# Softmax of the first two batches by tensor-engine transposes and row-spreading products

## The chip, the cores and the metric

The kernel runs on one core of one Trainium2 chip. TensorE (PE) multiplies, VectorE (DVE) and ScalarE (ACT) work elementwise, SyncE (SP) issues the DMAs; GpSimd (POOL) only fills constants. Each engine takes its instructions in the order written. The metric is the device time of one execution in microseconds, the median of several. A difference in percent is taken against the kernel before.

## The reference

```python
# x: (8 batches, 8 heads, 512 tokens, 64), state: (8, 8, 32 states, 64)
scores = matmul(x, state.T) / 8
a = exp(scores - scores.max(-1));  a /= a.sum(-1) + 1e-9     # softmax over the 32 states
xread = matmul(a, state)
scores2 = matmul(state, x.T) / 8                             # the same scores, transposed
a2 = exp(scores2 - scores2.max(-1)); a2 /= a2.sum(-1) + 1e-9 # softmax over the 512 tokens
sread = matmul(a2, x)
x = concat([xread, sread], tokens)          # (8, 544, 8*64) -> 4352 rows of 512
h = relu(x @ w_in1);  x = (s*h*h + b) @ w_out1               # 512 -> 2048 -> 512
h = relu(x @ w_in2);  out = (h*h) @ w_out2
```

## The kernel before

The matmuls of the two layers run in a rounded fp32 form, with each operand split in a high and a low part, so that a product takes three passes (high by high, high by low, low by high). Weights come as 64-bit words; ACT takes the magnitude of a piece (line 126), four DVE instructions turn it into fp32 (`to_f32`, lines 135 to 146), and the split follows.

**Attention.** Scores of a batch lie as two tiles (r = 0, 1) of 128 rows by 512 tokens; the rows are four heads by 32 states. So the softmax over tokens runs along a row, and the softmax over states across 32 rows. `att_exp` (line 351) does both: for the tokens a maximum along the row (355) and an exponential with its sum (360); for the states a 32 by 32 block transpose on DVE (358), a maximum (362), a subtraction (363) and an exponential (364). `att_norm` takes the sums and divides (369 to 376); `att_an` transposes the states' softmax back (382), rounds it to the high part (ACT, 384) and takes the low part (DVE, 387). `att_tp` transposes the tokens' softmax on PE (393), and `att_sr` (413) multiplies it by x.

**First layer.** The 64-wide product with the state is folded into the weights: S = state by w_in1 (`s_mm`, `s_first`), so that a step needs six passes `h <- aT, S` (line 448). A step (j, f) is one block of 128 hidden columns of batch j: `mm1` (six passes, 448), three ACT instructions for the squared relu and its high part (455 to 457), the low part on DVE (461), and two steps later `mm2` (twelve passes, 478), which sums into four PSUM banks. The order is steps 0 to 3 of batch 0, steps 4 to 7 of batch 1, then the other 12 of each, then the other batches.

**Order of the work.** It is written out by hand: before the loop over steps come the loads, the scores and softmax of batch 0 and the scores of batch 1; in step i come `mm1`, `early` (conversion of the piece of w_out1 or w_in1 that is due, the pieces of S, the low parts of the step before, relu, magnitudes of the next pieces), `mm2` of step i-2, and then what `at_step(i, fn, rank)` has put there, sorted by rank. Batch 1's softmax stands at steps 0 to 4 (list `first`): exponentials at 0, division at 1, transposes at 2, `att_sr` at 4. Batches 2 to 7 follow the list `calm`.

**Second layer.** Lines 630 to 720, PE products of another arrangement; the change does not touch them.

Of the kernel before, what the change touches and what calls it, by code (L numbers as in the profile page):

```python
# [40 lines left out]
P = 128  # L41
# [20 lines left out]
def attn_mlp2(ctx: ExitStack, tc: tile.TileContext, xT, xn, st, w_in1, w_out1, w_in2, w_out2, s_in, b_in, out):  # L62
# [40 lines left out]
    def x8(shape, name, dt=F32R):  # L103
        return xp.tile(shape, dt, tag="x", name=name)
# [65 lines left out]
    def piece(key, src, q, k):  # L170

        raw = load_piece(key, src, q, k)
        st = {}

        def mag():
            if key == "o1":
                st["v"] = vp.tile([P, 512], F32, tag="v", name="v")
            else:
                if k == 0:
                    V1[q] = w8([P, KD, 512], f"V{q}", F32)  # L180
                st["v"] = V1[q][:, :, k * P : (k + 1) * P]
            magnitude(st["v"], raw)

        def hi():
            nc.scalar.activation(out=w_tiles("o1", q)[0][:, k, :], in_=st["v"], func=ACTF.Copy)

        def lo():
            h, l = w_tiles("o1", q)
            nc.vector.tensor_tensor(out=l[:, k, :], in0=st["v"], in1=h[:, k, :].bitcast(F32), op=ALU.subtract)  # L189

        st.update(key=key, mag=mag, pair=lambda: (st["v"], raw), hi=hi, lo=lo)
        return st
# [137 lines left out]
            )  # L330
        xa[b] = [t, sb, None]

    def att_load_n(b):
        n = x8([P, S // P, DM], f"xn{b}", F32)
        nc.sync.dma_start(out=n, in_=xn[b].rearrange("(t p) d -> p t d", p=P))
        xa[b][2] = n

# [40 lines left out]
    def att_an(b, c, between=None):  # L378
        if c == 0:
            aT_t[b] = x8([P, 2, 2, S], f"aT{b}")  # L380
        an = an1.tile([P, S], F32, tag="an", name="an")
        nc.vector.transpose(out=an, in_=cur[b, c][1].rearrange("p a b -> p (a b)"))
        hi, lo = aT_t[b][:, 0, c, :], aT_t[b][:, 1, c, :]
        nc.scalar.activation(out=hi, in_=an, func=ACTF.Copy)
        if between:
            between()
        nc.vector.tensor_tensor(out=lo, in0=an, in1=hi.bitcast(F32), op=ALU.subtract)  # L387

    def att_tp(b, c):
        sc = cur[b, c][0]  # L390
        tp = pst(f"tp{b}{c}")
        for i in range(4):
            nc.tensor.transpose(out=tp[:, i * P : (i + 1) * P], in_=sc[:, i * P : (i + 1) * P], identity=ident)  # L393
        a2T = (at if b else op).tile([P, 4, P], F32, tag="t1" if b else "o", name="a2T")
        nc.scalar.copy(out=a2T, in_=tp.rearrange("p (a b) -> p a b", a=4))
        cur[b, c] = [a2T]

    def att_turn(b, c):
        att_an(b, c)
        att_tp(b, c)  # L400

    srp_t = {}

# [431 lines left out]
    def later(i, k, loader, rank=0):  # L835
# [12 lines left out]

    calm = ((att_sc, 0, 5), (att_exp, 0, 6), (att_exp, 1, 8), (att_norm, 0, 9), (att_norm, 1, 10),
            (att_an, 0, 11), (att_an, 1, 12), (att_tp, 0, 13), (att_tp, 1, 13), (att_sr, 0, 17), (att_put, 0, 17))  # L850
    first = ((att_exp, 0, 0), (att_exp, 1, 0), (att_norm, 0, 1), (att_norm, 1, 1), (att_turn, 0, 2),
             (att_turn, 1, 2), (att_sr, 0, 4), (att_put, 0, 4))
    rank = {att_sr: 0, att_tp: 0, att_sc: 0, att_put: 2, att_an: 3, att_turn: 3, att_exp: 5, att_norm: 5}
    for b in range(1, B):
        base = step(2, 0) + (b - 3) * NF if b > 1 else 0
        if b > 1:
            at_step(base + 1, lambda b=b: att_load(b), 6)
        at_step(base + 1, lambda b=b: att_load_n(b), 6)
        for fn, c, k in first if b == 1 else calm:
# [151 lines left out]
    with tc.manual_schedule():  # L1011
        make_identity(nc, ident)
        nc.scalar.activation(out=minus, in_=ident, func=ACTF.Copy, scale=-1.0)
        nc.gpsimd.memset(ones, 1.0)
        v0 = [piece("i1", w_in1, 0, 0)]
        att_load(0)
        v0 += [piece("i1", w_in1, 0, k) for k in range(1, VA)]
        nc.sync.dma_start(out=s_sb, in_=s_in.to_broadcast([P, 1]))
        nc.sync.dma_start(out=b_sb, in_=b_in.to_broadcast([P, 1]))
        v0[0]["mag"]()  # L1020
        to_f32(v0[0]["pair"]())
        att_sc(0, 0)
        s_first(0)
        att_exp(0, 0)
        s_first_lo(0)
        att_exp(0, 1)
        for p in v0[1:]:
            p["mag"]()
        att_load_n(0)
        att_load(1)  # L1030
        bring(0)
        bring(1)
        att_norm(0, 0)
        att_norm(0, 1)
        att_an(0, 0, lambda: to_f32(v0[1]["pair"]()))
        att_tp(0, 0)
        att_an(0, 1, lambda: to_f32(*[p["pair"]() for p in v0[2:]]))
        att_tp(0, 1)
        att_sc(1, 0)
# [64 lines left out]
```

## Time and profile before

| what | us |
|---|---|
| median of 3 runs (lowest, highest) | 1407.17 (1406.64, 1409.31) |
| the profiled execution's own time | 1405.25 |
| its span in the trace | 1403.5 |
| PE busy in the span | 1371.6 (98%) |
| DVE busy, ACT busy | 765.1 (55%), 759.1 (54%) |

The profile lists instructions by engine with their start, their duration and, in brackets, how long the engine had been idle before and what released it. A stretch's granted clock of TensorE is given as a share of 2.4 GHz (0.50 is 1.2 GHz). An fp32 matmul appears as two instructions. PEld is the loading of weights into PE. SPq is SyncE's queue of DMA issues.

### The profile page before, as it was taken

The numbers are of one execution on the slowest core, as the hardware profiler recorded it, in microseconds if no ns is written. First come the engines' busy times: TensorE is split into PE (matmuls) and PEld (weight loads), VectorE is DVE, ScalarE is ACT, GpSimd is POOL, SyncE is SP. The second block draws the span as 40 slices with busy tenths as digits, with TensorE's granted clock in tenths as the row PEclk, the third lists the DMA queues.
The fourth block names the chain that finished last, engine by engine and source line by source line (L and its number), as shares of the span: only waits on it lengthen the run. The fifth ranks groups of instructions, "written<-read, shape, count | busy, mean of one in ns | idle before, by whom it ended". The sixth has DMA issues, their size and how long they took to land.

```text
span 1403.5 us, 20210 instructions
## 1 busy us (share of the span) xinstructions
PE 1371.6 (98%) x7770; PEld 1159.5 (83%) x7770; DVE 765.1 (55%) x1495; ACT 759.1 (54%) x1492; POOL 0.7 (0%) x7
## 2 busy tenths in 40 slices
PE   4999999999999999999999999999999999999998
PEld 2677777777777777889988999988999988999897
DVE  7888645555565767345667544453444435343533
ACT  4877656656665656557655543363344335434543
POOL 0000000000000000000000000000000000000000
PEclk9999999999999999999999999999999999999999
DMA  7365232332414241302663655445445544543652
GB/s 239 120 220 184 90 112 73 116 113 85 145 49 143 83 147 60 113 0 98 215 225 138 189 162 160 119 149 158 119 125 172 165 120 120 165 128 108 216 157 68
DMA packets 88863, 188.48 MB, mean 134 GB/s; under 512 B 8640, under 2 KB 26048, under 8 KB 86208
## 3 DMA queue, kind: packets, MB, share of 16 engines
q1 hardware_dynamic: 88768, 187.21, 42.5%
q8 instruction: 61, 1.00, 0.3%
q14 instruction: 34, 0.28, 0.1%
HBM read 144.18 MB, written 42.99 MB: 133 GB/s over the span
## 4 chain that ended last, share of the span: by engine, by line
PE 95%; DVE 3%; ACT 1%; DMA 0%; issue 0%; SPq 0%
PE o L681 27%; PE acc L478 26%; PE m L636 24%; PE h L448 14%; PE S L260 2%; PE sr L413 1%; PE sc L260 1%; PE tp L393 0%; PE S L288 0%; DMA xT<-xT 0%; DVE m L362 0%; DVE t L376 0%; DVE t L363 0%; DVE V L141 0%; DVE V L146 0%
## 5 line engine op out<-in xcount | busy, mean ns | idle before, releaser
L478 PE MATMUL acc<-g,o1h 128*128 128x512 f32 (+1 forms) x1152 | 341.2, 379 | 0.0
L478 PEld LDWEIGHTS acc<-g,o1h 128*128 128x128 f32 x1152 | 211.4, 188 | 41.7 <-issue 2.0
L478 PE MATMUL acc<-g,o1l 128*128 128x512 f32 (+1 forms) x576 | 217.5, 378 | 0.4 <-DVE o1l L189 0.4
L448 PE MATMUL h<-aT,S 128*128 128x512 f32 x768 | 201.9, 397 | 6.2 <-DVE aT L387 3.5
L448 PEld LDWEIGHTS h<-aT,S 128*128 128x128 f32 x768 | 141.4, 189 | 60.9 <-issue 9.2
L636 PE MATMUL m<-xw 128*128 128x384 f32 (+1 forms) x1008 | 183.4, 328 | 2.3 <-DVE r L715 2.3
L636 PEld LDWEIGHTS m<-xw 128*128 128x128 f32 x1008 | 171.5, 188 | 10.0 <-DVE r L715 2.6
L649 ACT ACTIVATE sc<-sc 128x384 f32<-128x384 f32 (+1 forms) x144 | 72.8, 505 | 153.2 <-DVE sc L715 151.7
L461 DVE TENSOR_TENSOR g<-r,g 128x512 fp32r<-128x512 f32 (+1 forms) x144 | 94.8, 658 | 111.0 <-ACT g L457 111.0
L455 ACT ACTIVATE r<-h 128x512 f32<-128x512 f32 (+1 forms) x144 | 82.2, 570 | 124.5 <-PE h L448 123.2
L649 ACT ACTIVATE v<-m 128x384 f32<-128x384 f32 (+1 forms) x96 | 45.5, 474 | 152.8 <-PE m L636 152.2
L478 PEld LDWEIGHTS acc<-g,o1l 128*128 128x128 f32 x576 | 108.4, 188 | 21.1 <-DVE o1l L189 0.9
L681 PE MATMUL o<-o2h,xw('g', 0)_6295 128*128 128x512 f32 x364 | 121.2, 392 | 0.0
L681 PE MATMUL o<-o2h,xw('g', 1)_6296 128*128 128x512 f32 x364 | 121.1, 392 | 0.0
L681 PE MATMUL o<-o2h,xw('g', 2)_6297 128*128 128x512 f32 x360 | 119.7, 392 | 0.0
L715 DVE TENSOR_TENSOR v<-m,r 128x384 f32<-128x384 f32 (+1 forms) x48 | 25.7, 536 | 164.4 <-PE m L636 164.4
L636 PE MATMUL m<-xw,xw('odd', 0)_6176 128*128 128x384 f32 (+1 forms) x576 | 107.4, 328 | 0.8 <-DVE t L715 0.8
L636 PEld LDWEIGHTS m<-xw,xw('odd', 0)_6176 128*128 128x128 f32 x576 | 98.3, 188 | 5.0 <-DVE t L715 1.2
L456 ACT ACTIVATE r<-r 128x512 f32<-128x512 f32 (+1 forms) x144 | 87.7, 609 | 4.6
L457 ACT ACTIVATE g<-r 128x512 fp32r<-128x512 f32 (+1 forms) x144 | 87.6, 609 | 4.6
L111 DVE TENSOR_TENSOR S<-S,S 128x512 fp32r<-128x512 f32 x54 | 34.8, 686 | 91.4 <-ACT S L110 91.4
L636 PE MATMUL m<-xw,xw('odd', 1)_6177 128*128 128x384 f32 (+1 forms) x432 | 79.3, 327 | 0.0
(146 smaller groups left out, 1893.5 us busy)
## 6 DMA issues: line engine op xcount, KB each, us to landing
xw<-w2s SPq DMA_DIRECT2D x140, 256.0 KB, 2.8
xw('odd', 0)_6176<-w2s SPq DMA_DIRECT2D x20, 1024.0 KB, 4.9
xw('odd', 1)_6177<-w2s SPq DMA_DIRECT2D x20, 768.0 KB, 4.3
i1r<-w_in SPq DMA_DIRECT2D x16, 512.0 KB, 5.0
xn<-xn SPq DMA_DIRECT2D x8, 1024.0 KB, 8.8
o1r<-w_out SPq DMA_DIRECT2D x16, 512.0 KB, 4.8
x<-ot SPq DMA_DIRECT2D x32, 256.0 KB, 3.0
i2r<-w_in SPq DMA_DIRECT2D x16, 512.0 KB, 5.3
```

Source lines behind the costliest of these rows:

```text
L111: nc.vector.tensor_tensor(out=lo, in0=src, in1=hi.bitcast(F32), op=ALU.subtract)
L260: nc.tensor.matmul(out=outs[r][k * NS : (k + 1) * NS], lhsT=state[rows, r, k, :], rhs=moving(rows, k), start=True, stop=True, skip_group_c ...
L448: nc.tensor.matmul(out=hp, lhsT=l_, rhs=r_, start=(i == 0), stop=(i == len(ops) - 1))
L455: nc.scalar.activation(out=r, in_=hp, func=ACTF.Relu)
L456: nc.scalar.activation(out=r, in_=r, func=ACTF.Square)
L457: nc.scalar.activation(out=g[:, 0], in_=r, func=ACTF.Copy)
L461: nc.vector.tensor_tensor(out=g[:, 1], in0=r, in1=g[:, 0].bitcast(F32), op=ALU.subtract)
L478: nc.tensor.matmul(out=o, lhsT=l_, rhs=r_, start=(opens and i == 0), stop=(closes and i == 2))
L636: nc.tensor.matmul(out=o, lhsT=w[:, a, k, :], rhs=x[:, b, k, :], start=(start and k + a + b == 0), stop=(k + a == 2), skip_group_check=True,)
L649: nc.scalar.activation(out=c, in_=src, func=func)
L681: nc.tensor.matmul(out=acc2[t], lhsT=l_, rhs=r_, start=(fa == 0 and e == 0), stop=(fa == NF - 1 and e == 2))
L715: add = lambda o, x, y: nc.vector.tensor_tensor(out=o, in0=x, in1=y, op=ALU.add)
```

## The change

For batches 0 and 1, `att_sc`, `att_exp`, `att_norm` and `att_an` are replaced by new functions; batches 2 to 7 keep the old ones. The scores are copied out unscaled. Per tile, `soft_max` transposes them on PE to 128 tokens by (4 chunks, 4 heads, 32 states), and DVE takes the negated maximum over states from PSUM, 16 numbers per token. `to_rows` spreads these over the rows again by 16 fp32 products per tile, whose weights are one column broadcast 32 times and whose moving operand is the identity; in `soft_exp` they add onto the scores in PSUM, from which ACT takes the exponential. `soft_sum` sums over states by products with a matrix `heads` of ones, 4 columns wide, once per batch; DVE inverts. `soft_norm` spreads the inverse by `to_rows`, multiplies on DVE and rounds on ACT; `soft_lo` takes the low part. The softmax over tokens moves to `soft_state`, which stands at step 0 for batch 0 and at step 3 for batch 1; `att_tp` and `att_sr` follow at steps 1 and 2 for batch 0 and 4 and 6 for batch 1. Loads of x for batch 1 and the first pieces of w_out1 are issued before batch 0's second copy of x.

```diff
+    heads = const.tile([P, KD], F32, name="heads")
...
+    def soft_sc(b):
+        t, sb, _ = xa[b]
+        sps = [pa.tile([P, 512], F32, tag="acc", name=f"sc{b}{r}") if b else pst(f"sc{b}{r}") for r in range(2)]
+        per_head(sps, sb, lambda rows, k: t[rows, k, :])
+        for r, sp in enumerate(sps):
+            pool, tag = (at, "sc") if b else (op, "o")
+            sc = pool.tile([P, S], F32, tag=tag, name="sc")
+            nc.scalar.activation(out=sc, in_=sp, func=ACTF.Copy)
...
+    def soft_max(b, r):
+        sc = cur[b, r][0]
+        tp = pa.tile([P, 512], F32, tag="acc", name=f"tm{b}{r}")
+        for i in range(4):
+            nc.tensor.transpose(out=tp[:, i * P : (i + 1) * P], in_=sc[:, i * P : (i + 1) * P], identity=ident)
+        m = cur["m", b, r] = sm.tile([P, 16, 1], F32, tag="m1", name="m1")
+        nc.vector.tensor_reduce(
+            out=m[:, :, 0], in_=tp.rearrange("p (a s) -> p a s", s=NS), axis=AX.X, op=ALU.max, negate=True
+        )
+    def to_rows(out, v, start):
+        for i in range(4):
+            for k in range(KD):
+                nc.tensor.matmul(
+                    out=out[k * NS : (k + 1) * NS, i * P : (i + 1) * P],
+                    lhsT=v[:, KD * i + k, :].to_broadcast([P, NS]),
+                    rhs=ident, start=start, stop=True, skip_group_check=True,
+                )
+    def soft_exp(b, r):
+        sp = cur.pop(("ps", b, r))
+        to_rows(sp, cur.pop(("m", b, r)), False)
+        e = cur["e", b, r] = at.tile([P, S], F32, tag="t1", name="e")
+        nc.scalar.activation(out=e, in_=sp, func=ACTF.Exp, scale=scale)
+    def soft_sum(b):
+        pt = pst(f"sum{b}")[:, : 32]
+        for r in range(2):
+            for i in range(4):
+                c0 = 16 * r + KD * i
+                nc.tensor.matmul(
+                    out=pt[:, c0 : c0 + KD], lhsT=cur["e", b, r][:, i * P : (i + 1) * P], rhs=heads,
+                    start=True, stop=True, skip_group_check=True,
+                )
+        for r in range(2):
+            s = cur["s", b, r] = sm.tile([P, 16, 1], F32, tag="s1", name="s1")
+            nc.vector.tensor_scalar(
+                out=s[:, :, 0], in0=pt[:, 16 * r : 16 * r + 16], scalar1=1e-9, scalar2=None, op0=ALU.add
+            )
+            nc.vector.reciprocal(out=s, in_=s)
+    def soft_norm(b, r):
+        pt = pst(f"inv{b}{r}") if b else pa.tile([P, 512], F32, tag="acc", name=f"inv{b}{r}")
+        to_rows(pt, cur.pop(("s", b, r)), True)
...
+        nc.vector.tensor_tensor(out=e, in0=e, in1=pt, op=ALU.mult)
+        nc.scalar.activation(out=aT_t[b][:, 0, r, :], in_=e, func=ACTF.Copy)
+    def soft_lo(b, r):
+        hi, lo = aT_t[b][:, 0, r, :], aT_t[b][:, 1, r, :]
+        nc.vector.tensor_tensor(out=lo, in0=cur.pop(("e", b, r)), in1=hi.bitcast(F32), op=ALU.subtract)
+    def soft_state(b, r):
+        (sc,) = cur[b, r]
+        nm2 = sm.tile([P, 1], F32, tag="nm2", name="nm2")
+        nc.vector.tensor_reduce(out=nm2, in_=sc, axis=AX.X, op=ALU.max, negate=True)
+        s2 = sm.tile([P, 1], F32, tag="s2", name="s2")
+        nc.vector.tensor_scalar(out=nm2, in0=nm2, scalar1=scale, scalar2=None, op0=ALU.mult)
+        nc.scalar.activation(out=sc, in_=sc, func=ACTF.Exp, bias=nm2, scale=scale, accum_out=s2)
+        nc.vector.tensor_scalar(out=s2, in0=s2, scalar1=1e-9, scalar2=None, op0=ALU.add)
+        nc.vector.reciprocal(out=s2, in_=s2)
+        nc.scalar.activation(out=sc, in_=sc, func=ACTF.Copy, scale=s2)
...
-    first = ((att_exp, 0, 0), (att_exp, 1, 0), (att_norm, 0, 1), (att_norm, 1, 1), (att_turn, 0, 2),
-             (att_turn, 1, 2), (att_sr, 0, 4), (att_put, 0, 4))
...
+        n0 = x8([P, S // P, DM], "xn0", F32)
+        att_load(1)
+        bring(0)
+        att_load_n(0, n0)
+        bring(1)
         v0[0]["mag"]()
         to_f32(v0[0]["pair"]())
-        att_sc(0, 0)
+        soft_sc(0)
+        soft_max(0, 0)
+        soft_max(0, 1)
         s_first(0)
-        att_exp(0, 0)
+        v0[1]["mag"]()
+        soft_exp(0, 0)
+        soft_exp(0, 1)
+        to_f32(v0[1]["pair"]())
+        v0[2]["mag"]()
+        soft_sum(0)
         s_first_lo(0)
-        att_exp(0, 1)
-        for p in v0[1:]:
-            p["mag"]()
...
+        soft_norm(0, 0)
+        soft_norm(0, 1)
+        soft_lo(0, 0)
+        soft_lo(0, 1)
+        v0[3]["mag"]()
+        to_f32(*[p["pair"]() for p in v0[2:]])
+        soft_sc(1)
         for p in stage[0]:
             p["mag"]()
-        at_step(1, lambda: att_sr(0, 0), 0)
-        at_step(2, lambda: att_put(0, 0), 0)
+        for r in range(2):
+            at_step(0, lambda r=r: soft_max(1, r), -1)
+            at_step(0, lambda r=r: soft_state(0, r), 1)
+            at_step(1, lambda r=r: soft_exp(1, r), -1)
+            at_step(1, lambda r=r: att_tp(0, r), 0.5)
+            at_step(2, lambda r=r: soft_norm(1, r), -1)
+            at_step(2, lambda r=r: soft_lo(1, r), -1)
+            at_step(3, lambda r=r: soft_state(1, r), 1)
+            at_step(4, lambda r=r: att_tp(1, r), 1)
+        at_step(1, lambda: soft_sum(1), 0)
+        for b, i in ((0, 2), (1, 6)):
+            at_step(i, lambda b=b: att_sr(b, 0), 0)
+            at_step(i + 1, lambda b=b: att_put(b, 0), 0)
```

## Rows read from the trace of the kernel before

**Rows 1.** Waits of PE from 70 us to the end (total us, times, longest)

```profile
PE m L636 <- DVE r L715: 2.3, 1, 2.3
```

**Rows 2.** Waits of PE in the first 70 us

```profile
PE sc L260 <- DMA xT<-xT: 7.7, 1, 7.7
PE tp L393 <- ACT sc L373: 7.1, 1, 7.1
```

**Rows 3.** Stretches of the first 50 us: length, then busy time by engine, clock

```profile
0.00:8.00 8.00, 0.26 (x4) 0.22 (x8) 2.24 (x4) 2.25 (x3) 0.74 (x7) 1.00 0.70 224
8.00:20.00 12.00, 4.51 (x33) 1.08 (x25) 8.06 (x18) 6.90 (x15) 0.00 (x0) 1.00 0.91 324
20.00:30.00 10.00, 5.78 (x29) 2.75 (x30) 9.79 (x20) 4.29 (x8) 0.00 (x0) 0.86 0.32 97
30.00:40.00 10.00, 7.96 (x75) 5.19 (x74) 9.66 (x16) 6.99 (x17) 0.00 (x0) 0.67 0.73 256
40.00:50.00 10.00, 9.17 (x101) 7.07 (x100) 8.93 (x23) 9.47 (x18) 0.00 (x0) 0.96 0.34 97
```

**Rows 4.** DVE instructions of the first 130 us by shape (busy us, mean ns)

```profile
L358 DVE STREAM_TRANSPOSE t<-sc 128x512 f32<-128x512 f32 x4 | 2.8, 701 | 0.0
...
L355 DVE TENSOR_REDUCE nm<-sc 128x1 f32<-128x512 f32 x4 | 2.7, 680 | 4.1 <-ACT sc L348 4.1
...
L375 DVE RECIPROCAL s<-s 128x16 f32<-128x16 f32 x4 | 1.0, 253 | 0.1
```

**Rows 5.** PE in order of time: start, us; the same work at two clocks

```profile
10.84 1.08 PE L288 MATMUL S<-V,st 128*32 128x128 f32 x16
...
20.07 1.94 PE L393 MATMUL tp<-ident,sc 128*128 128x128 f32 x8 [7.06 <-ACT sc L373]
...
48.63 1.06 PE L393 MATMUL tp<-ident,sc 128*128 128x128 f32 x8 [0.83 <-DVE sraw L423]
...
61.39 0.64 PE L288 MATMUL S<-V,st 128*32 128x128 f32 x16
```

**Rows 6.** Weight loads of the column sums `cs` (min/median/max ns, first and last start)

```profile
L231 PEld LDWEIGHTS cs<-ones,wsum x8: 187/192/192, 557.2 to 558.1; 128*128 128x128 f32 x8
```

**Rows 7.** ACT in order of time, steps 0 and 1

```profile
33.72 0.38 ACT L296 ACTIVATE S<-S 128x256 fp32r<-128x256 f32 x1 [0.47 <-PE S L288]
...
36.89 0.91 ACT L306 ACTIVATE S<-S 128x256 fp32r<-128x256 f32 x3
37.68 0.73 ACT L360 ACTIVATE sc<-sc,nm 128x512 f32<-128x512 f32 x1
38.30 0.21 ACT L360 ACTIVATION_READ_ACCUMULATOR sc<-sc,nm 128x1 f32 x1
...
40.13 0.59 ACT L455 ACTIVATE r<-h 128x512 f32<-128x512 f32 x1
...
43.11 1.09 ACT L275 ACTIVATE S<-S 128x512 fp32r<-128x512 f32 x2
```

**Rows 8.** DVE in order of time: weight conversions and a low part

```profile
25.26 0.72 DVE L135 TENSOR_SCALAR V<-V 128x512 f32<-128x512 f32 x2
...
28.97 0.68 DVE L387 TENSOR_TENSOR aT<-an,aT 128x512 fp32r<-128x512 f32 x1
...
37.15 0.42 DVE L135 TENSOR_SCALAR v<-v 128x512 f32<-128x512 f32 x1
...
39.40 0.69 DVE L189 TENSOR_TENSOR o1l<-v,o1h 128x512 fp32r<-128x512 f32 x1
```

**Rows 9.** PE in order of time: first, third and fifth `mm1`, `att_sr`, a low product

```profile
29.71 1.22 PE L448 MATMUL h<-aT,S 128*128 128x512 f32 x2 [3.16 <-DVE aT L387]
...
42.95 1.66 PE L448 MATMUL h<-aT,S 128*128 128x512 f32 x6
...
53.64 1.52 PE L448 MATMUL h<-aT,S 128*128 128x512 f32 x6
...
57.81 2.06 PE L413 MATMUL sr<-a2T,xn 128*64 128x32 f32 x64
...
63.12 0.50 PE L478 MATMUL acc<-g,o1l 128*128 128x512 f32 x1 [0.42 <-DVE o1l L189]
```

More of the change, by code (lines that the diff above doesn't have):

```diff
@@ L331, in att_load, with att_load_n @@
         xa[b] = [t, sb, None]
-    def att_load_n(b):
-        n = x8([P, S // P, DM], f"xn{b}", F32)
+    def att_load_n(b, n=None):
+        n = x8([P, S // P, DM], f"xn{b}", F32) if n is None else n
         nc.sync.dma_start(out=n, in_=xn[b].rearrange("(t p) d -> p t d", p=P))
@@ L349, in att_sc @@
             cur[b, r] = [sc]
+    def soft_sc(b):
[6 more added lines that the diff above has]
+            nc.scalar.activation(out=sc, in_=sp, func=ACTF.Copy)
+            cur[b, r] = [sc]
+            cur["ps", b, r] = sp
@@ new lines, in soft_norm @@
+    def soft_norm(b, r):
+        pt = pst(f"inv{b}{r}") if b else pa.tile([P, 512], F32, tag="acc", name=f"inv{b}{r}")
+        to_rows(pt, cur.pop(("s", b, r)), True)
+        if r == 0:
+            aT_t[b] = x8([P, 2, 2, S], f"aT{b}")
+        e = cur["e", b, r]
+        nc.vector.tensor_tensor(out=e, in0=e, in1=pt, op=ALU.mult)
[3 more added lines that the diff above has]
+        nc.vector.tensor_tensor(out=lo, in0=cur.pop(("e", b, r)), in1=hi.bitcast(F32), op=ALU.subtract)
@@ L396, in att_tp @@
         cur[b, c] = [a2T]
-    def att_turn(b, c):
-        att_an(b, c)
-        att_tp(b, c)
     srp_t = {}
@@ L850, in attn_mlp2 @@
             (att_an, 0, 11), (att_an, 1, 12), (att_tp, 0, 13), (att_tp, 1, 13), (att_sr, 0, 17), (att_put, 0, 17))
-    first = ((att_exp, 0, 0), (att_exp, 1, 0), (att_norm, 0, 1), (att_norm, 1, 1), (att_turn, 0, 2),
-             (att_turn, 1, 2), (att_sr, 0, 4), (att_put, 0, 4))
-    rank = {att_sr: 0, att_tp: 0, att_sc: 0, att_put: 2, att_an: 3, att_turn: 3, att_exp: 5, att_norm: 5}
+    rank = {att_sr: 0, att_tp: 0, att_sc: 0, att_put: 2, att_an: 3, att_exp: 5, att_norm: 5}
     for b in range(1, B):
@@ L858, in attn_mlp2 @@
         at_step(base + 1, lambda b=b: att_load_n(b), 6)
-        for fn, c, k in first if b == 1 else calm:
+        for fn, c, k in calm if b > 1 else ():
             at_step(base + k, lambda fn=fn, b=b, c=c: fn(b, c), rank[fn])
@@ L1014, in attn_mlp2 @@
         nc.gpsimd.memset(ones, 1.0)
+        nc.gpsimd.memset(heads, 0.0)
+        for k in range(KD):
+            nc.gpsimd.memset(heads[k * NS : (k + 1) * NS, k : k + 1], 1.0)
         v0 = [piece("i1", w_in1, 0, 0)]
@@ L1019, in attn_mlp2 @@
         nc.sync.dma_start(out=b_sb, in_=b_in.to_broadcast([P, 1]))
+        n0 = x8([P, S // P, DM], "xn0", F32)
[3 more added lines that the diff above has]
+        bring(1)
         v0[0]["mag"]()
         to_f32(v0[0]["pair"]())
-        att_sc(0, 0)
+        soft_sc(0)
+        soft_max(0, 0)
+        soft_max(0, 1)
         s_first(0)
-        att_exp(0, 0)
-        s_first_lo(0)
-        att_exp(0, 1)
-        for p in v0[1:]:
-            p["mag"]()
[L1029 to L1039, printed above, removed]
+        v0[1]["mag"]()
[4 more added lines that the diff above has]
+        soft_sum(0)
+        s_first_lo(0)
+        soft_norm(0, 0)
[5 more added lines that the diff above has]
+        soft_sc(1)
         for p in stage[0]:
             p["mag"]()
-        at_step(1, lambda: att_sr(0, 0), 0)
-        at_step(2, lambda: att_put(0, 0), 0)
+        for r in range(2):
[11 more added lines that the diff above has]
+            at_step(i + 1, lambda b=b: att_put(b, 0), 0)
         gs = {}
```

## The prediction

> **What bounds the kernel now.** I read the waits of PE first. After 70 us PE waits for almost nothing (2.3 us in one place, in the second layer [rows 1]): from there the time is PE's own work, which the change leaves alone. So it can only move the moment at which PE has got through the first steps. In the first 70 us PE waits 7.7 us for the first x and 7.1 us for the softmax of batch 0 [rows 2]. The stretches say who holds it up: from 20 to 40 us DVE is busy 19.45 of 20 us, PE 13.74 [rows 3]. Up to 48 us the chain of waits runs over DVE without a hole, and the transposes, maxima, divisions and weight conversions stand in one line there. From about 49 us PE is full. PE's clock is low in this part: 0.86 of 2.4 GHz from 20 to 30 us, 0.67 from 30 to 40, 0.96 from 40 to 50 [rows 3]; 0.50 is 1.2 GHz. The column reads 1.00 before 20 us, but 16 small products took 1.08 us at 10.84 and 0.64 at 61.39 [rows 5], so the lower level holds there too.
>
> **What goes from DVE and what comes to PE.** Per tile (batch, r; four in all) DVE did eight operations of 512 columns, 0.67 to 0.70 us each, the first and one more shown, two inversions and three small ones [rows 4]: 6.3 us. Now it does four (maximum of the transposed scores, multiplication, low part, maximum along the row) at about 0.7, with PSUM sources in two, and the small ones: 3.7. DVE gets back 2.6 x 4 = 10.4 us. ACT's list is the same kind by kind (copy, two exponentials, division, rounding, copy of the transposed tile): nothing gained or lost in sum.
>
> PE gets new work. `to_rows` is 16 fp32 products, 32 instructions of the shape that `s_first` runs 16 of (32-column weights, 128 moving columns): twice 0.64 less some overlap, 1.2 us at full clock and 2.2 at the low one [rows 5]. It runs twice per tile, eight times: 9.6 us at full clock. The bounds: 0.6 if the repeated weight column made the pair of instructions as cheap as one, 3.4 if the four 32-column strips did not run side by side (32 x 0.107); I take 1.2, for the row has the same shape. The sums are 8 products with 128-column weights and 4 moving columns per batch. The nearest row is `cs`, 128-column weights and 2 moving columns: eight instructions start from 557.2 to 558.1, 1.0 us [rows 6]; sixteen take 2.0 per batch, 4.0 in all; at half, if the loading overlapped better, 2.0. The transposes, eight per batch, take 1.06 at full clock, 1.94 at the low [rows 5]: 2.1. Sum: 15.7 us of PE work. And the room: PE was not busy in 50 - 27.7 = 22.3 of the first 50 us [rows 3], of which 7.7 is the wait for x and stays: 14.6. The work that comes is as large as the hole it goes into. That alone takes most of a gain away.
>
> **Placing it, batch 0.** Times on the trace's scale. Scores end at 10.9; copy 0.6, four transposes at the low clock 1.0, the second four to 13.5 (DVE's maxima beside them), `s_first` to 14.5. The first `to_rows` ends at 16.6 (low). PE has been busy since 11.6, and from 40 to 50 us the row is back at 0.96 after ten in which PE was busy for 7.96 [rows 3], so I let the clock rise here; the second ends at 17.8, its exponential at 18.4, the sums (the first half beside it) at 19.5, two small DVE steps at 20.0, then 1.2 + 1.2 of products, multiplication 0.7, rounding 0.6, low part 0.7: the last operand of the first `mm1` at 24.7, `mm1` done at 25.5. Before it ended at 30.9 [rows 9]. PE is 5.4 us ahead here.
>
> DVE is not. The conversion of pieces 2 and 3 of w_in1 stands behind the second low part: 24.7 against 25.26 [rows 8]. 3.7 us for the two, 2.3 for the first piece of w_out1 (what a piece took from 37.15 to 39.40 [rows 8]): 30.7; then the two maxima of batch 1, 32.0. ACT goes from the third piece of S to the three low pieces in 4.1 us [rows 7] and ends at 33.4 instead of 37.8.
>
> **The new stop.** `soft_state` is a chain that changes engine three times: maximum and scaling on DVE 0.85, exponential with its sum on ACT 0.73 + 0.21 [rows 7], addition and inversion on DVE 0.35, division on ACT. The old code put other DVE work between; here the addition is the next DVE instruction, and behind it stand the second tile's maximum, the conversion of the second piece of w_out1 and the low parts that `mm2` needs. At step 0: maximum to 32.9; ACT is free at 33.4, exponential to 34.3; inversion 34.7; second maximum 35.6, exponential 36.5, inversion 36.9. DVE spends 4.9 us on 2.4 of work, and the conversion starts at 36.9 against 37.15 [rows 8]: batch 0's lead is gone.
>
> PE at step 1: `mm1` and two `to_rows` end at 36.6. Then the sums wait for the exponentials of batch 1. On ACT these stand behind the division of `soft_state` (37.6) and step 1's relu group, magnitude and rounding (3.0, from 40.13 to 43.11 before [rows 7]): 40.6, exponentials at 41.1 and 41.6. Behind the waiting sums are queued `att_tp`, S of batch 1 and the next `mm1`. Sums to 43.1, transposes beside DVE's inversions to 44.2, S 1.0: third `mm1` at 45.2, against 42.95 [rows 9], 2.3 behind, and the idle 4.5 us before may lower the clock once more, up to 2.
>
> From the third to the fifth `mm1` it took 10.7 us [rows 9], with 0.83 idle and 0.8 of transposes in it [rows 5]. Both go; two `to_rows` (2.4) and batch 0's `att_sr` (2.06 [rows 9], in the old order ahead of the third `mm1`) come: 13.5, fifth `mm1` at 58.7, 5 behind.
>
> **The sum.** The fourth `mm1` ends at 55.9, and at step 3 `soft_state` of batch 1 stops DVE again: maximum from 56.8; on ACT the exponential stands behind the relu group and two magnitudes, until 59.8; second maximum, second exponential until 62.1, free at 62.5. Then two pieces (3.8), a low part (0.6), one piece (2.3) and the low part that `mm2` of step 3 needs (0.6): 69.8. Before, that product started at 63.12 [rows 9]: 6.7 late. Batch 1's `att_sr`, 2.0, was done before that point and now comes at step 6: 8.7 us in all. Steps behind this are PE's work alone, and DVE's share of them is unchanged. So 1405.25 + 8.7 = 1414 for the profiled execution, which is 1.9 under the median; on the median 1407.17 + 8.7 = 1416. With the added idle at a lower clock 2 more, with the clock up a few us earlier 2 less, with half-price products and sums 4 less: 1411 to 1420 is this case's own range.
>
> Costed at nothing: the five memsets (POOL works 0.74 us of the span and POOL is waited for by nothing [rows 3]); the loads' new order on SP, where x of batch 1 and the first w_out1 piece go ahead of the second copy of x, which `att_sr` now wants only after 50 us; the second w_out1 piece waits on SP for the conversion of piece 1, with later weight loads behind it, and lands 15 us before use. If a load were late, its wait would show on ACT's magnitudes.
>
> **Rivals.** (1) *DVE's relief carries through*, the other side: the 10.4 us count, the stops at `soft_state` are short because ACT is free, PE's holes take the new work. Best case: 14.6 of room less 15.7 of work, plus what the low clock cost, 0.14 x 5.8 + 0.33 x 8.0 + 0.04 x 9.2 = 3.8 us [rows 3], a gain of 2.7; with `to_rows` at half, 7.5. It decides at the conversion of the second w_out1 piece: it must start near 33, not 37. About 1402. For it: DVE is the chain until 48. Against: no room on PE. (2) *The costs cancel*: stops as I say, but products, sums and transposes at the lower bounds, the clock up early: within 2.8 us, about 1408. (3) *No stop on DVE*: ACT reaches the exponentials early, so each pair costs DVE 2.4 instead of 5; the third `mm1` then starts 2.5 us sooner, the fifth is 2.6 late, and step 4's transposes add 0.9: 3.5 late by PE's order alone, 1411. (4) *Low clock throughout the stretch*: the rise that I put at 16.6 does not come, and the wait at step 1 keeps it down until 42. Batch 0 costs 1.0 more in each of the three later `to_rows` and, in the ratio of 1.94 to 1.06 [rows 5], 1.7 in the sums, about 5 on top of 8.7: 1421. The Trainium skill, "TensorE: Matmul & The Clock Gate", section "Part 4: PE-mode transpose", says that transposes do not count as activity for the clock; by that rule this rival gains weight, and no row here shows transposes alone. (5) *The strips don't overlap*: 3.4 instead of 1.2 per `to_rows`, 8 x 2.2 = 18 more: 1434. Rows 5 speak against it.
>
> **Chances.** Forecast 0.54, (1) 0.07, (2) 0.11, (3) 0.14, (4) 0.11, (5) 0.03. Two tenths of a percent, 2.8 us, is about what a measurement of this kernel can tell from no change. Faster holds (1) without its small gains, 0.06; the same holds (2) and the rest of (1), 0.12; slower the others, 0.82. The range leaves out (1), (2) and (5), 0.21, less the part of (2) at its edge: 1409.5 to 1422.
>
> **What would show it.** In the profile after: DVE idle released by ACT's exponential at `soft_state`, twice at step 0 and twice at step 3, 1 to 2 us each; PE idle ahead of the first sums of batch 1, released by ACT, near 4 us; eight groups of 32 products at 1.2 us (2.2 at the low clock); a first `mm1` some 5 us earlier and a ninth some 9 later. I am wrong if the second w_out1 piece is converted well before 36 us, if the products cost half, or if PE waits for something after 90 us.

## The result, and the profile after

| | before | after |
|---|---|---|
| median, us (lowest, highest; 4 runs each) | 1406.91 (1406.42, 1409.31) | 1418.36 (1416.96, 1419.06) |
| the profiled execution, its span | 1405.25, 1403.5 | 1417.9, 1416.1 |
| PE busy | 1371.6 | 1388.9 |
| DVE busy, ACT busy | 765.1, 759.1 | 755.2, 760.1 |

The ratio is 1.0084, with a 95% interval of 1.0071 to 1.0098: slower by 11.4 us. DVE has 9.9 us less to do, and the kernel is longer.

The three longest waits of PE in the first 100 us of the kernel after (total us, times, longest) answer [rows 2]. The 7.1 us in front of batch 0's transposes are gone; a wait for batch 1's exponentials and one for a low part of w_out1 have come. From 88 us on there are only the two waits of the second layer that the kernel before has too (2.3 and 0.8), so the change makes its loss before 88 us.

```profile
PE sc L261 <- DMA xT<-xT: 6.9, 1, 6.9
PE sum L396 <- ACT e L389: 4.7, 1, 4.7
PE acc L555 <- DVE o1l L190: 2.1, 1, 2.1
```

Stretches of the kernel after, as in [rows 3] (busy us of PE, PEld, DVE, ACT, POOL, then the granted clock). From 30 to 60 us DVE, the full engine of before, is busy less than half of the time; the clock falls to 0.61 behind the stretch in which PE is busy for only 4.98 of 10 us.

```profile
20.00:30.00 10.00, 8.03 (x98) 5.37 (x91) 8.95 (x17) 6.65 (x13) 0.00 (x0) 0.84 0.45 151
30.00:40.00 10.00, 4.98 (x76) 3.53 (x75) 5.59 (x15) 8.29 (x18) 0.00 (x0) 0.84 0.70 246
40.00:50.00 10.00, 10.00 (x50) 7.28 (x51) 4.00 (x10) 3.66 (x7) 0.00 (x0) 0.61 0.19 57
50.00:60.00 10.00, 10.00 (x156) 8.41 (x155) 4.82 (x9) 6.06 (x11) 0.00 (x0) 1.00 0.01 2
...
70.00:80.00 10.00, 9.44 (x54) 7.18 (x54) 7.33 (x14) 6.50 (x13) 0.00 (x0) 0.83 0.64 202
```

PE in order of time (start, us) answers [rows 5, 6, 9]. `to_rows` is L379 (64 instructions are two calls), the sums L396, `mm1` L525, `att_sr` L490, the low product L555. The last line is the ninth `mm1`.

```profile
11.39 1.06 PE L369 MATMUL tm<-ident,sc 128*128 128x128 f32 x8 [0.80 <-ACT sc L361]
...
12.85 1.93 PE L379 MATMUL sc<-ident,m 128*32 128x128 f32 x64
14.72 1.94 PE L396 MATMUL sum<-heads,e 128*128 128x4 f32 x16
...
17.21 3.50 PE L379 MATMUL inv<-ident,s 128*32 128x128 f32 x64 [0.33 <-DVE s L402]
...
21.66 2.06 PE L525 MATMUL h<-aT,S 128*128 128x512 f32 x6
...
38.88 3.58 PE L396 MATMUL sum<-heads,e 128*128 128x4 f32 x16 [4.73 <-ACT e L389]
42.32 1.95 PE L474 MATMUL tp<-ident,sc 128*128 128x128 f32 x8
44.20 1.96 PE L261 MATMUL S<-V,st 64*32 64x512 f32 x16
46.09 2.41 PE L525 MATMUL h<-aT,S 128*128 128x512 f32 x6
...
59.74 1.52 PE L525 MATMUL h<-aT,S 128*128 128x512 f32 x6
...
70.56 0.50 PE L555 MATMUL acc<-g,o1l 128*128 128x512 f32 x1 [2.06 <-DVE o1l L190]
...
79.78 2.06 PE L490 MATMUL sr<-a2T,xn 128*64 128x32 f32 x64
...
86.93 1.55 PE L525 MATMUL h<-aT,S 128*128 128x512 f32 x6
```

The first `mm1` is done at 23.7 us, 7 us ahead of before. The fifth starts 6.1 us behind (59.74, 53.64 before), the low product that `mm2` of step 3 needs 7.4 behind (70.56, 63.12), the ninth `mm1` 11.15 behind (86.93, 75.78 before). The kernel before has the ninth at:

```profile
75.78 1.55 PE L448 MATMUL h<-aT,S 128*128 128x512 f32 x6
```

From there the distance stays for a long time: the column sums `cs`, which began at 557.2 [rows 6], begin at 568.2, 11.0 later. At the end of the profiled executions it is 12.6 (spans of 1416.1 and 1403.5). The other 1.6 us arise in the second layer, behind a wait of 2.3 us that both kernels have (first two lines before, last two after):

```profile
714.43 1.33 PE L636 MATMUL m<-xw 128*128 128x384 f32 x6 [2.25 <-DVE r L715]
...
717.91 2.27 PE L636 MATMUL m<-xw 128*128 128x384 f32 x12
725.49 1.33 PE L713 MATMUL m<-xw 128*128 128x384 f32 x6 [2.26 <-DVE r L792]
...
730.54 2.25 PE L713 MATMUL m<-xw 128*128 128x384 f32 x12
```

The same products take 3.48 us before and 5.05 after, where the granted clock was 0.70 from 725 to 730 us; before it stayed at 1.00, and so it did behind this wait in the profiles of e6 and e9 below. That this level depends on the change is not shown, so the 11.15 us of the first 88 us are the figure to explain.

DVE in order of time: `soft_state` (L424 to L429) of both batches, between them the waits for PE. The brackets are DVE's idle time. It answers [rows 8]: the second piece of w_out1 is converted at 34.56, 2.6 us ahead of before, and DVE's lead is then lost in waits of 4.41 and 6.16 us for PE.

```profile
32.28 0.15 DVE L428 TENSOR_SCALAR s<-s 128x1 f32<-128x1 f32 x1 [1.37 <-ACT sc L427]
...
34.29 0.15 DVE L428 TENSOR_SCALAR s<-s 128x1 f32<-128x1 f32 x1 [0.88 <-ACT sc L427]
...
34.56 0.41 DVE L136 TENSOR_SCALAR v<-v 128x512 f32<-128x512 f32 x1
...
42.49 0.17 DVE L402 TENSOR_SCALAR s<-sum 128x16 f32<-128x16 f32 x1 [4.41 <-PE sum L396]
...
52.86 0.69 DVE L413 TENSOR_TENSOR e<-e,inv 128x512 f32<-128x512 f32 x1 [6.16 <-PE inv L379]
...
60.96 0.15 DVE L428 TENSOR_SCALAR s<-s 128x1 f32<-128x1 f32 x1 [1.85 <-ACT sc L427]
...
62.96 0.15 DVE L428 TENSOR_SCALAR s<-s 128x1 f32<-128x1 f32 x1 [0.88 <-ACT sc L427]
```

DVE's shapes, as in [rows 4]: the maximum and the multiplication read PSUM and cost what those of before cost that read SBUF.

```profile
L413 DVE TENSOR_TENSOR e<-e,inv 128x512 f32<-128x512 f32 x4 | 2.7, 686 | 8.9 <-PE inv L379 8.9
...
L371 DVE TENSOR_REDUCE m<-tm 128x16 f32<-128x512 f32 x4 | 2.6, 684 | 4.3 <-PE tm L369 4.3
```

ACT, as in [rows 7]: batch 1's exponentials (L389) stand behind the last division, the relu group, a magnitude and a rounding.

```profile
34.73 0.72 ACT L430 ACTIVATE sc<-sc,s 128x512 f32<-128x512 f32 x1 [0.48 <-DVE s L429]
35.36 0.58 ACT L532 ACTIVATE r<-h 128x512 f32<-128x512 f32 x1
...
38.25 1.06 ACT L389 ACTIVATE e<-sc 128x512 f32<-128x512 f32 x2
```

### The profile page after: what moved, and what is told of

It is laid out like the page before. It is cut to its first block, busy times and chain, and to the rows that moved or that the text cites. A ratio compares the mean times of both kernels' runs of the same rounds, so it can differ in the third digit from the quotient of the medians.

```text
span 1416.1 us, 20812 instructions
## 1 busy us (share of the span) xinstructions
PE 1388.9 (98%) x8074; PEld 1175.7 (83%) x8074; DVE 755.2 (53%) x1483; ACT 760.1 (54%) x1492; POOL 1.2 (0%) x12
## 4 chain that ended last, share of the span: by engine, by line
PE 96%; ACT 2%; DVE 1%; DMA 0%; issue 0%; SPq 0%; ACTq 0%; DVEq 0%
PE o L758 26%; PE acc L555 26%; PE m L713 23%; PE h L525 14%; PE S L261 2%; PE sr L490 1%; PE S L289 1%; PE sc L261 1%; PE tp L474 0%; DMA xT<-xT 0%; PE sum L396 0%; PE inv L379 0%; ACT sc L427 0%; DVE V L142 0%; ACT sc L430 0%
## 5 line engine op out<-in xcount | busy, mean ns | idle before, releaser
L555 PE MATMUL acc<-g,o1h 128*128 128x512 f32 (+1 forms) x1152 | 341.8, 380 | 0.5 <-ACT o1h L186 0.5
L555 PEld LDWEIGHTS acc<-g,o1h 128*128 128x128 f32 x1152 | 211.7, 188 | 42.4 <-issue 2.0
L555 PE MATMUL acc<-g,o1l 128*128 128x512 f32 (+1 forms) x576 | 218.0, 378 | 2.1 <-DVE o1l L190 2.1
L525 PE MATMUL h<-aT,S 128*128 128x512 f32 x768 | 201.7, 398 | 0.3 <-ACT S L307 0.3
L525 PEld LDWEIGHTS h<-aT,S 128*128 128x128 f32 x768 | 142.0, 190 | 54.8 <-issue 11.7
L555 PEld LDWEIGHTS acc<-g,o1l 128*128 128x128 f32 x576 | 108.7, 189 | 23.0 <-DVE o1l L190 2.5
L758 PE MATMUL o<-o2h,xw('g', 0)_6455 128*128 128x512 f32 x364 | 121.4, 393 | 0.0
L758 PE MATMUL o<-o2h,xw('g', 1)_6456 128*128 128x512 f32 x364 | 121.1, 392 | 0.0
L758 PE MATMUL o<-o2h,xw('g', 2)_6457 128*128 128x512 f32 x360 | 120.8, 396 | 0.0
L713 PE MATMUL m<-xw,xw('odd', 0)_6336 128*128 128x384 f32 (+1 forms) x576 | 107.4, 328 | 0.8 <-DVE t L792 0.8
L713 PEld LDWEIGHTS m<-xw,xw('odd', 0)_6336 128*128 128x128 f32 x576 | 98.3, 188 | 5.0 <-DVE t L792 1.2
L713 PE MATMUL m<-xw,xw('odd', 1)_6337 128*128 128x384 f32 (+1 forms) x432 | 79.3, 327 | 0.0
```

What stands on the lines that cost most here:

```text
L525: nc.tensor.matmul(out=hp, lhsT=l_, rhs=r_, start=(i == 0), stop=(i == len(ops) - 1))
L555: nc.tensor.matmul(out=o, lhsT=l_, rhs=r_, start=(opens and i == 0), stop=(closes and i == 2))
L713: nc.tensor.matmul(out=o, lhsT=w[:, a, k, :], rhs=x[:, b, k, :], start=(start and k + a + b == 0), stop=(k + a == 2), skip_group_check=True,)
L758: nc.tensor.matmul(out=acc2[t], lhsT=l_, rhs=r_, start=(fa == 0 and e == 0), stop=(fa == NF - 1 and e == 2))
```

## The experiments

Two theories were set against each other. *Stops*: the time is lost where an engine waits in the new order (DVE in `soft_state`, PE in front of the sums, the low clock behind that). *Load*: PE's added products, 13.6 us at full clock, exceed the idle time that they fill, wherever the waits are. All are compared with the kernel before on the same chip; a ratio of 1.0010 is 1.4 us, and the intervals reach 1 to 2 us to either side. Differences between two runs on different chips are given as they were measured; by the ratios they come out up to 0.9 us otherwise.

**One batch alone.** e1 gives batch 1 its old softmax (`att_exp` to `att_tp` by the list `first`), e2 gives batch 0 its old one.

```diff
# e1
-        soft_sc(1)
+        att_sc(1, 0)
...
-            at_step(0, lambda r=r: soft_max(1, r), -1)
...
# e2
-        soft_sc(0)
+        att_sc(0, 0)
...
-        for b, i in ((0, 2), (1, 6)):
+        for b, i in ((0, 1), (1, 6)):
```

> Batch 0 by the new softmax, batch 1 by the old one. Two theories of the 11.4 us. Stops: they are waits that PE meets because another engine's list is held up (PE's sums of batch 1 behind ACT's exponentials, with the clock that falls after it; DVE held by soft_state at step 3), so they belong to batch 1: 1408 to 1410, 1 to 3 over the kernel before, which is what soft_state of batch 0 costs DVE. Load: PE has no room for the added work, 13.6 us at full clock, half of it per batch: 1412 to 1414.

> Batch 0 by the old softmax, batch 1 by the new one. Stops: both stops are still there, the one at step 1 about as long (PE has its spread products done some 2 us after the first scores' exponentials could start, ACT gets to them at 43): 1415 to 1418. Load: half of the work, 1412 to 1414.

e1: 1409.12, ratio 1.0024 (1.0012 to 1.0035). e2: 1418.57, ratio 1.0087 (1.0072 to 1.0102). e1 is where Stops has it, e2 0.6 us above that and far from Load. Half of the added products is in each, but batch 1 alone costs as much as the whole change, and batch 0 alone 3.3 us. The two do not add: in after, batch 0's lead pays for a part of batch 1's loss. e2's PE waits show the same stop at the low part as after. In front of the sums it waits only 1.8 us, where I had expected about as much as the 4.7 of after, and its third `mm1` starts at 47.58:

```profile
PE acc L555 <- DVE o1l L190: 2.1, 1, 2.1
PE sum L396 <- ACT e L389: 1.8, 1, 1.8
```

```profile
47.58 1.66 PE L525 MATMUL h<-aT,S 128*128 128x512 f32 x6
```

That is 4.6 us behind before [rows 9], and ahead of it stand 5.4 us of batch 1's new products (1.56, 1.95 and 1.92 us). So where batch 0 gives no lead, the added products themselves cost time up to here; e2's time fits Stops, but its trace has a good part of Load in it.

**The stop in `soft_state`.** e3 cuts it behind the exponential; addition, inversion and division come a step later.

```diff
+        cur["half", b, r] = s2
+    def soft_state_b(b, r):
+        (sc,) = cur[b, r]
+        s2 = cur.pop(("half", b, r))
         nc.vector.tensor_scalar(out=s2, in0=s2, scalar1=1e-9, scalar2=None, op0=ALU.add)
...
+            at_step(1, lambda r=r: soft_state_b(0, r), 0.4)
+            at_step(4, lambda r=r: soft_state_b(1, r), 0.9)
```

> soft_state in two halves: maximum and exponential where it stood, addition, inversion and division one step later, ahead of att_tp, so that DVE has other work between. Stops: DVE converts the second w_out1 piece 3 us sooner, ACT's exponentials of batch 1 come 2.3 us sooner and PE's wait halves; the 2.6 us that PE waits at step 5 go: 1409 to 1412. Load: no work is taken off PE, so the wait only moves: 1415 to 1418.

1413.93, ratio 1.0055 (1.0040 to 1.0070): 4.4 us under after (4.1 by the ratios), between the two expectations. PE's wait for the low part is gone; in its place PE waits for the division that now comes late. So the stop is real, and a part of what its end gave went into a new wait:

```profile
PE tp L479 <- ACT sc L435: 3.3, 2, 1.8
PE sum L396 <- ACT e L389: 2.2, 1, 2.2
```

**The wait of the sums.** e4 puts the sums of batch 1 behind the transposes and S of step 1; e5 does this and e3's cut; e6 leaves the order and puts 20 products of the identity with itself, whose output nobody reads, ahead of the sums, so that PE works where it waited.

```diff
-        at_step(1, lambda: soft_sum(1), 0)        # e4, e5
+        at_step(1, lambda: soft_sum(1), 1.5)
...
+        for _ in range(20 * b):                   # e6
+            nc.tensor.matmul(
+                out=bank[:, P : 2 * P], lhsT=ident, rhs=ident, start=True, stop=True, skip_group_check=True
+            )
```

> In step 1 the sums of batch 1 go behind att_tp of batch 0 and S of batch 1, which wait for nothing then; nothing else moves. Stops: PE's wait of 4.7 us shrinks to under 3, and the sums, transposes and S run at the full clock: third mm1 4 to 5 us sooner, 1413 to 1415. Load: PE's list is as long as before, at most 2 us: 1416 to 1418.

> The two edits of the split soft_state and of the sums placed last, together (alone 4.4 and 3.3 us under the changed kernel). If they take away two different stops: the sum, 7 to 8 under the changed kernel, 1410 to 1411, and what is left over the kernel before, 3 to 5 us, is PE's added work that found no idle time. If both act on one wait: 4 to 5 under it, 1413 to 1414.

> Ahead of the sums of batch 1, 20 products of the identity with itself that nothing reads, 4.3 us at full clock, fill the wait of 4.7 us at step 1; the result is the same. The clock theory: the 4 us that the sums, transposes, S and third mm1 lose at the low clock after the wait come back: 3 to 4 under the changed kernel, 1414 to 1415.5. If the clock has no part in it or the fill overruns the wait: 1418 to 1419.

e4: 1415.05, ratio 1.0064 (1.0049 to 1.0079), at the upper end of what Stops gave. e5: 1412.18, ratio 1.0042 (1.0029 to 1.0056), between the two cases that I had named. e6: 1413.99, ratio 1.0053 (1.0038 to 1.0069): more work on PE, and 4.4 us less time. Its stretch of the sums ran at full clock (0.61 in after), its third `mm1` began at 43.01 instead of 46.09, and the wait for the low part stayed. The filling products took 4.76 us there (I had put 4.3).

```profile
43.01 1.65 PE L530 MATMUL h<-aT,S 128*128 128x512 f32 x6
```

```profile
30.00:40.00 10.00, 9.91 (x116) 9.08 (x116) 4.71 (x12) 7.33 (x16) 0.00 (x0) 0.83 0.60 206
40.00:50.00 10.00, 10.00 (x130) 7.68 (x130) 4.69 (x11) 5.90 (x11) 0.00 (x0) 1.00 0.18 56
```

e4 and e5 shortened (to 2.7 us) or removed the wait in front of the sums and kept the low clock, against what I had expected of e4; in e5 it is the lowest of all there, 0.51:

```profile
40.00:50.00 10.00, 10.00 (x45) 7.68 (x30) 4.00 (x10) 3.57 (x7) 0.00 (x0) 0.51 0.07 15
```

**All stops together.** e10 has e3's cut and e6's products, and puts batch 0's transposes at step 2 and `att_sr` at step 3.

```diff
-            at_step(1, lambda r=r: att_tp(0, r), 0.5)
+            at_step(2, lambda r=r: att_tp(0, r), 0.5)
-        for b, i in ((0, 2), (1, 6)):
+        for b, i in ((0, 3), (1, 6)):
```

> Both batches new, with the split soft_state of e3 and the 20 filling products of e6 together; batch 0's transposes go to step 2 and its att_sr to step 3, so that the wait for the division that e3 showed (3.3 us) goes too. Stops: the gains of e3 (4.4) and e6 (4.4) are separate terms and add: 1409 to 1411, ratio 1.002 to 1.003; what is left is load. Load: they overlap, and the added 13.6 us of PE work leaves 5 to 7 us whatever is done about the waits: 1412 to 1414, ratio 1.004 to 1.0055, with hardly any PE wait after the first 10 us but those of 1 us or less.

1409.78, ratio 1.0017 (1.0008 to 1.0026): 8.6 us under after, where 4.4 + 4.4 = 8.8. So the gains add, with the third edit, the later transposes and `att_sr`, in the sum; it was not run alone. By the times 2.4 us (0.0017 of 1407) of the loss are left. By the traces it is more: e10's ninth `mm1` starts at 80.99, 5.2 us behind before, against 11.15 in after. So the stops make up at least half of the loss. What is left is not all load either. With e3's cut ACT has batch 1's exponentials done at 37.20, and the sums stand behind the filling products until 40.61, so that the filling itself overran by some 3.4 us:

```profile
36.14 1.06 ACT L389 ACTIVATE e<-sc 128x512 f32<-128x512 f32 x2
```

```profile
40.61 1.85 PE L401 MATMUL sum<-heads,e 128*128 128x4 f32 x16
...
80.99 1.55 PE L535 MATMUL h<-aT,S 128*128 128x512 f32 x6
```

A shorter filling was not tried. The longest waits of its PE behind the first load:

```profile
PE S L289 <- DVE V L147: 1.9, 1, 1.9
PE h L535 <- ACT S L307: 1.8, 1, 1.8
```

**The price of load.** e8 issues the products that spread batch 1's inverse three times, four more calls of `to_rows` in a stretch in which PE has no idle time.

```diff
+        s = cur.pop(("s", b, r))
+        for _ in range(1 + 2 * b):
+            to_rows(pt, s, True)
```

> The spread products of the inverse of batch 1 are issued three times with the same result: 4 more calls at 0.94 us. They stand at step 2, where PE has no idle time, and the fourth mm1, the relu group, the exponentials and the stop of DVE at step 3 all follow behind them: 3.8 over the changed kernel, 1421.5 to 1423, by either theory; it is the price of the load where PE is full. If the wait at step 5 hid part of it: 1419 to 1420.

1421.85, ratio 1.0111 (1.0097 to 1.0124): 3.5 us over after. In its trace the six calls take 5.45 us, where two took 1.95, so 3.50 more:

```profile
50.46 5.45 PE L379 MATMUL inv<-ident,s 128*32 128x128 f32 x192
```

Within the interval of some 2 us, load costs its full price where PE is full. So it is a cost beside the stops; after's own two calls of this kind, 1.95 us, stand in that stretch too. By e3, e6 and e10 it does not set the size of the loss alone.

**Batch 0 alone, in another order.** e7 and e9 keep batch 1 old and put batch 0's softmax over tokens into the idle time ahead of the loop, its transposes before the first `mm1`, its `att_sr` at step 1. In e7 I set `soft_state(0, 0)` ahead of `soft_max`; its exponential overwrites the scores that PE is to transpose. e9 sets it behind, converts the third piece of w_in1 before the spread inverse is needed, and copies batch 0's state read at the end of step 1.

```diff
         soft_sc(0)                                # e9
         soft_max(0, 0)
         soft_max(0, 1)
...
         soft_exp(0, 1)
+        soft_state(0, 0)
+        soft_state(0, 1)
...
+        soft_state_b(0, 0)
+        soft_state_b(0, 1)
+        v0[3]["mag"]()
+        to_f32(v0[2]["pair"]())
         soft_norm(0, 0)
...
+        att_tp(0, 0)
+        att_tp(0, 1)
+        at_step(1, lambda: att_sr(0, 0), 0)
+        at_step(1, lambda: att_put(0, 0), 6)
```

> Batch 0 new, batch 1 old, and batch 0's softmax over tokens woven into the idle time of DVE and ACT before the loop, its transposes before the first mm1, its product with x at step 1 as in the kernel before. Stops: nothing holds DVE at step 0 any more; it reaches batch 1's softmax 2.9 us sooner than in the kernel before, and PE's new work for batch 0, 6.8 us, lies in PE's idle time: 2 to 3.5 under the kernel before, ratio 0.9975 to 0.9985. Load: half of the added work stays, 3 to 5 over the kernel before.

> Batch 0 new with the tokens' softmax before the loop, as in e7, but behind the transposes for the maximum, so that PE does not wait 2.6 us for the exponential that overwrites the scores; the third piece of w_in1 is converted in DVE's idle time before the spread inverse comes; the copy of batch 0's state read goes to the end of step 1, where batch 1's transposes waited 2.5 us for it. Batch 1 old. Stops: with both waits gone the lead of batch 0 reaches the third mm1 and PE's order behind it: the ninth mm1 at 73 to 75 us against 75.78 before, ratio 0.9975 to 0.999 (1403 to 1405). Load: batch 0's added 6.8 us of products eat what the waits gave: ninth mm1 at 76 or later, ratio 1.000 to 1.001.

e7: 1406.52, ratio 1.0004 (0.9995 to 1.0012), a miss: its transposes waited 2.61 us, the exponential that overwrites the scores standing before them, and batch 1's transposes later waited 2.5 us for the copy of the state read:

```profile
12.90 1.07 PE L369 MATMUL tm<-ident,sc 128*128 128x128 f32 x8 [2.61 <-ACT sc L427]
```

e9: 1403.38 against 1406.82, ratio 0.9971 (0.9959 to 0.9982), faster than both kernels. Its DVE converts the second piece of w_out1 at 32.43 (37.15 before, [rows 8]), its third `mm1` starts at 35.48 (42.95 before [rows 9]), and its ninth at 72.18, 3.6 us before the old one:

```profile
32.43 0.42 DVE L136 TENSOR_SCALAR v<-v 128x512 f32<-128x512 f32 x1
```

```profile
35.48 2.77 PE L534 MATMUL h<-aT,S 128*128 128x512 f32 x6
...
72.18 1.55 PE L534 MATMUL h<-aT,S 128*128 128x512 f32 x6
```

Is the gain that of the copy, which has nothing to do with the softmax? e12 is the kernel before with that edit alone.

```diff
-        at_step(2, lambda: att_put(0, 0), 0)
+        at_step(1, lambda: att_put(0, 0), 6)
```

> The kernel before with one edit that e9 also has and that has nothing to do with the softmax: the copy of batch 0's state read goes to the end of step 1 instead of step 2. Batch 1's transposes waited 0.83 us for it. If e9's gain of 4 us is from batch 0's new softmax, this gives 0 to 1 us, ratio 0.9993 to 1.000; if it is from this wait and the order behind it, 2 us or more, ratio under 0.9985.

1405.78, ratio 0.9999 (0.9990 to 1.0008): no, not from the copy alone. What is left is batch 0's new softmax in e9's order; how much of the gain is from the order of `soft_state` and how much from the earlier conversion was not taken apart. Nor was the new order of the loads, which e9 keeps, tried alone. In the traces PE waits for a load only at the first x, 7.7 us before and 6.9 in e9. This wait lies between 6.5 and 8.0 us in the profiles of the kernels that have the new order, so up to 0.9 of the 3.6 us belongs to these two executions.

**Both batches in that order.** e11 is e9 with batch 1 new, `soft_state` cut as in e3, and batch 0's `att_sr` ahead of batch 1's sums in place of e6's products.

```diff
-        att_sc(1, 0)
+        soft_sc(1)
...
+        at_step(1, lambda: att_sr(0, 0), -0.5)
+            at_step(3, lambda r=r: soft_state(1, r), 1)
+            at_step(4, lambda r=r: soft_state_b(1, r), 0.9)
+            at_step(4, lambda r=r: att_tp(1, r), 1)
```

> Batch 0 as in e9, batch 1 new as well, with the split soft_state of e3; instead of e6's filling products, batch 0's att_sr stands ahead of batch 1's sums at step 1 and covers their wait. Stops: without the waits batch 1's part gives no loss either; PE's 6.8 us of new products for it meet the idle time that e9 still has in the first 55 us (1.9, 1.8) and the low clock from 30 to 50 us: ratio 0.996 to 0.999 (1401 to 1405), at best equal to e9. Load: PE was busy for 10.0 of the 10 us from 30 to 40 in e9, so that most of the 6.8 us comes on top: e9 plus 4 to 6, ratio 0.9995 to 1.0015 (1406 to 1409).

1411.07, ratio 1.0029 (1.0019 to 1.0040), above both expectations, and nearer to that of Load. The trace shows a stop all the same: with no wait in front of the sums the fifth `mm1` starts at 50.64, 3.0 us ahead of before and only 0.6 behind e9's (50.06), although all of batch 1's new products are done by then (its transposes of the tokens' softmax, 1.0 us, are still to come). Up to there Load is not borne out. Then PE waits for `soft_state`'s division, whose inversion stands on DVE behind two pieces' conversions (52.5 to 56.3 us), and the `mm1` behind it takes 2.73 instead of 1.66.

```profile
50.64 1.52 PE L530 MATMUL h<-aT,S 128*128 128x512 f32 x6
...
58.02 1.73 PE L479 MATMUL tp<-ident,sc 128*128 128x128 f32 x8 [3.14 <-ACT sc L435]
59.40 2.73 PE L530 MATMUL h<-aT,S 128*128 128x512 f32 x6
```

Its ninth `mm1` starts at 77.92, 5.7 us behind e9's. The wait and the slow instructions behind it (0.7 in the transposes, 1.1 in the `mm1`) are 4.9 of that. Whether batch 1's new softmax would pay with this wait gone too stays open; it wasn't tried.

## Why the prediction was right

The mechanism and the sign held. The sum was 8.7 us; it came out as 11.1 at the ninth `mm1` and as 11.4 between the medians, and 1416 as 1418.36.

- *DVE gets back 10.4 us*: 9.9 by the busy times. *PE's added work 15.7*: 13.6, with `to_rows` at 0.95 us (I had 1.2), the sums at 1.94 per batch (2.0), the transposes at 1.06 each (as put).
- *Batch 0 ahead by 5.4 us*: 7.2 (23.7 against 30.9 [rows 9]). The clock was up at 11.39 already, where I had put the rise at 16.6. That is a matter of the execution: in e3, e5 and e10, whose instructions are the same up to there, the same eight transposes took 1.94, not 1.06. In after the lower level came a little later, in the two calls at 17.21 (3.50). (The steps that I listed up to the last operand add up to 24.4, not 24.7.)
- *`soft_state` stops DVE twice a step*: it does, 1.37 and 0.88 at step 0, 1.85 and 0.88 at step 3. At step 0 it was over 2.3 us sooner than I had put it (34.56, not 36.9), since ACT was less behind. A conversion well before 36 us was one of my signs of being wrong, and here my working did fail: batch 0's lead was not gone at this point, 2.6 us of it were left.
- *PE waits 4.5 us for batch 1's exponentials*: 4.73. Third `mm1` 46.09 (45.2), fifth 59.74 (58.7), low product 70.56 (69.8): 7.4 late where I had 6.7. The chain holds, step by step, with about a microsecond between.
- *`att_sr` behind that point, 2.0*: 2.06.
- The term that was mis-sized is the clock. I had put it beside the sum, as "2 more". Behind the wait of the sums the lower level costs 1.64 in the sums, 0.89 in the transposes, 0.87 in S, 0.75 in the third `mm1`, 4.15 in all. This is inside the 7.4. That the 7.4 is still near my 6.7 is luck in part: the sums started at 38.88, where I had ACT's first exponential of batch 1 at 41.1, so the chain was 2.2 us sooner there, and the products behind it were cheaper. Behind the wait for the low part the clock is 0.83 from 70 to 80 us, by that share some 1.7 us, and these are on top, with `att_sr`: 7.4 + 2.1 + 1.7 = 11.2, which is the ninth `mm1`'s 11.15.
- What I did not see: DVE's two waits for PE. I had carried DVE's lead nowhere, so they did not change the sum, but they are why a lead of 2.6 us at 34.56 was worth nothing: the conversions of the next pieces stand behind the inversion and behind `soft_norm`, and PE was at the lower clock there.

Of the rivals, (1) named the point from which it decides, a conversion of the second w_out1 piece near 33 us, and about 1402 us; e9, with half of the change, has it at 32.43 and takes 1403.4. (2) fell by the time. (3) fell: both stops are there. (4) fell in its size, but half of it came: the lower level held from the sums into the third `mm1`, and its 1.7 us for the sums is 1.64 measured. For batch 0 its clock did not stay low: the transposes at 11.39 us took 1.06, the full rate of [rows 5], right behind 3.7 us of scores and 0.8 of idle time, though the two calls at 17.21 ran low. The rule of the Trainium skill ("TensorE: Matmul & The Clock Gate", "Part 4: PE-mode transpose"), that transposes do not count as activity, is neither shown nor refuted by that, since other products ran before; no run here shows transposes alone. (5) fell: 64 instructions took 1.93.

## What to carry to other kernels

Work moved from the full engine to an idle one is only worth what the queue behind it lets through: look for the first instruction of the new chain that waits for another engine, and at what stands behind it in that engine's order. A chain that changes engine several times belongs into a stretch where its engines idle, or cut in two with other work between; but what the later half releases has then to be later too, or the wait only changes its place (e3, e11). An idle matmul engine can cost twice, in the wait and in the lower clock behind it, so real work (or, for want of it, useless work) in front of a waiting matmul can be worth more than a shorter wait.

## What was not expected of the hardware

- 20 useless products of 128 columns made the kernel 4.4 us faster (e6), with PE busy for 9.91 of 10 us where it had been for 4.98, and a granted clock of 1.00 instead of 0.61 in the next 10 us.
- The 32 instructions of `to_rows`, whose weights are one column broadcast, took 0.95 us at full clock, 30 ns each; the 16 of `s_first`, of the same shape, took 0.64, 40 ns each [rows 5]. The length of the group makes the difference, not the broadcast column: 48 of `s_first` in one row took 1.54 in e9, 32 ns each, and six calls of `to_rows` in e8 5.45, 28 ns each. My 1.2 came from doubling a short group. At the low clock two calls took 3.50.
- DVE's maximum and multiplication with a PSUM operand took 684 and 686 ns, the operations from SBUF 680 and 701 [rows 4].
- The granted clock of the same stretch differs between kernels that take the same time: e12 has 0.67 from 20 to 30 us and 0.77 from 40 to 50, where before has 0.86 and 0.96 [rows 3]. The same instructions also meet either level in different executions: batch 0's eight transposes took 1.06 us in after, e4 and e6 and 1.94 in e3, e5 and e10, and behind the second layer's wait the clock was 0.70 in after and 1.00 before. So a low clock in one profile is a reason only where an edit moves it, and the time with it, as in e6.
